# Batch 2 transposed by the DMA crossbar in the start of a fused attention and ReGLU kernel, with a new written order

## The chip, the core and the metric

The kernel runs on one core of a Trainium2 chip. A core has a matrix engine (TensorE, PE in the profile, with its weight loads as PEld), a vector engine (DVE), a scalar engine (ACT), GpSimd (POOL) and SyncE (SP). Each of them takes its instructions in order and waits on semaphores. DMA transfers are issued from SP, ACT and POOL and are carried by 16 DMA engines. Matmuls read SBUF and write PSUM, which has eight banks of 128 x 512 fp32. The metric is the device time of the program in microseconds; lower is better.

## The reference

Two functions are chained. The first is a cross attention between the tokens `x` (8 batches, 8 heads, 512 tokens, 64 features) and a state of 32 rows per head; both directions are computed, and their outputs are concatenated along the rows. The second is a ReGLU feed-forward layer (512 to 1536 to 512).

```python
scores = scale * np.matmul(x, state.transpose(0, 1, 3, 2))     # then softmax over the state rows
xread = np.matmul(a, state)
scores2 = scale * np.matmul(state, x.transpose(0, 1, 3, 2))    # then softmax over the tokens
sread = np.matmul(a2, x)
attn = np.concatenate([xread, sread], axis=2)                  # (B, H, S + Ns, D), to rows of H * D
gate = np.maximum(attn @ w_gate, 0.0)
out = gate * (attn @ w_val) @ w_out
```

Inputs and output are fp32; the kernel computes its matmuls in bf16.

## The kernel before

For a batch `b` the product of the attention with the weights is regrouped: `U[b]` = state times `w_gate` and `w_val` (256 x 1536 each), so that gate and value are `U` times the attention weights. The steps of one batch are these.

- `x` is loaded and brought to bf16 in `xb`. A load by GpSimd can convert on the way (`x_load`, L430, word `dx`); a plain load goes to an fp32 tile `xf` (`x_dma`, L100, word `df`), which an engine then converts (`x_conv`, L144). `x_next` (L438, word `xn`) converts both halves on GpSimd and issues a crossbar transpose from SP into `xT` (`x_trans_dma`, L166).
- `xT` can also come from TensorE: `x_T2` (L188, word `xT2`) makes 16 transposes into PSUM, and `x_out2` (word `xo2`) copies them to SBUF.
- The states come in groups `g` of two batches. `state_conv` (L119, word `stc`) writes them with the unused heads zeroed, in two halves. Then either `state_T` (L127, word `stT`, four transposes on TensorE) and `state_out` (L141, word `sto`) bring them into `stT`, or `state_T_dma` (L133, by the crossbar, from SP) and `state_out_dma` (L137).
- `att_sc` (L201, word `sc`) makes the scores of half the heads, `att_exp` (`ex`) the exponential on ACT, `att_sum` (`nr`) and `att_scale` (`nx`) the softmax on DVE, giving `a_sn`.
- `a_sn` is transposed into `ANS[b]`: by `att_T` (L239, `aT`) and `att_out` (L257, `ao`) through PSUM, or by `att_aT_dma` (L234) from SP.
- `c_unit` and `u_unit` (words `c`, `u`) compute pieces of `U`; `c_out` and `u_out` (`co`, `uo`) copy them out of PSUM.
- `gv` (L331) makes gate and value of one slice of 128 hidden features, four matmuls into two PSUM banks; `relu` on ACT (`re`) and `mult` on DVE (`mu`) give a slice of `hsb`.
- `out_part` (L400, word `o`) is a third of the second layer's matmuls for 128 tokens; `fin_x` (L371, word `of`) copies the sum out and stores it from SP.
- The other direction is `sr_mm` (`sr`), `sr_norm` (`sn`) and a copy of x with a column of ones (`x_pad`, `xp`, on GpSimd); its result is transposed by the crossbar (`sr_T_dma`) and goes through a loop of its own at the end.

The kernel sets its own order. The first 28 slices (all of batches 0 and 1, four of batch 2) follow the string `program` (L456 to L483), a list of words: the name of a step, its arguments, the engine of a copy, and after `@` the PSUM banks. The order of the words is the order in which each engine gets its instructions. `spin` words are matmuls on zeros into a bank of their own, placed in the start. GpSimd's DMA words are, in order: x of batch 1 (the tail of batch 0 stands ahead of the string), fourteen pieces of the two weights (`dw`), x of batch 2, the states (`ds`), the two halves of `w_out` (`do`), and x of batch 3.

From slice 28 on a loop takes over (`first`, L518): one `gv`, `relu`, `mult` and one output part for each slice, and at fixed slices the attention of the next batch, its `U`, the loads and the crossbar transposes. This loop is the same text in both kernels. The output parts lag 18 slices behind.

Buffers that matter here: two of `xf`, four of `xb`, two of `xT`, two of `a_sn`, three of `ANS`, four of the output tile.

Of the kernel before, what the change touches and what calls it, by code (L numbers as in the profile page):

```python
# [16 lines left out]
def kernel(  # L17
# [9 lines left out]
    nc = tc.nc  # L27

    B, H, S, D = x.shape
# [40 lines left out]
    stT = const.tile([128, B, NJ, 64], BF16, name="stT")  # L70
# [6 lines left out]
    xf, xb, xT, e_sn, a_sn, ANS, U, hsb, sr_sb = {}, {}, {}, {}, {}, {}, {}, {}, {}  # L77
    copy = {"act": nc.scalar.copy, "dve": nc.vector.tensor_copy, "pool": nc.gpsimd.tensor_copy}

    given, turn = [], {"r": 0, "o": 1}  # L80

    def bank(name, kind="r"):

# [12 lines left out]
    def state_dma(eng, lo, hi):  # L96
        src = state.rearrange("(g b) h (m i) d -> (b h m) g i d", b=2, i=4)
        eng.dma_start(out=st_f[:, lo // 2:hi // 2], in_=src[:, lo // 2:hi // 2])

    def x_dma(b, engs):  # L100
        xf[b] = xin.tile([128, H, NC, D], FP32, name="xf", tag="xf")
        n = H // len(engs)
        for i, eng in enumerate(engs):
            src = x[b, i * n:(i + 1) * n].rearrange("h (p c) d -> p h c d", c=NC)
            eng.dma_start(out=xf[b][:, i * n:(i + 1) * n], in_=src)
# [262 lines left out]
    def out_rows(b, tsub):  # L368
        return out[b * SP: b * SP + S].rearrange("(p q) m -> q p m", q=NC)[tsub]

    def fin_x(b, tsub, eng="act"):  # L371
        o_sb = opool.tile([128, d_model], FP32, name="o_sb", tag="o_sb")
        copy[eng](out=o_sb, in_=held["o", b, tsub])  # L373
        n = 2 if b == B - 2 and tsub < 2 else 1
        for i in range(n):
            rows = slice(128 // n * i, 128 // n * (i + 1))
            nc.sync.dma_start(out=out_rows(b, tsub)[rows], in_=o_sb[rows])
# [26 lines left out]
    def out_piece(b, i):  # L404
        out_part(b, i)
        if i % 3 == 2:
            fin_x(b, i // 3)
# [37 lines left out]
    def spin(n, cols=512):  # L445
        for i in range(n):
# [2 lines left out]


    steps = {"spin": spin, "stc": state_conv, "stT": state_T, "sto": state_out, "xc": x_conv_pair, "xT": x_T, "xT2": x_T2, "xo2": x_out2, "on": lambda: nc.gpsimd.memset(xa[:, :, :, D:D + 1], 1.0), "dw": w_load, "dx": x_load, "ds": lambda: state_dma(nc.gpsimd, 2, B), "do": wo_dma,
             "df": lambda b: x_dma(b, (nc.gpsimd,)), "xo": x_out,
             "sc": att_sc, "ex": att_exp, "nr": att_sum, "nx": att_scale, "aT2": att_T2, "ao2": att_out2, "aT": att_T, "ao": att_out,
             "c": c_unit, "co": c_out, "u": u_unit, "uo": u_out, "gv": gv, "re": relu, "mu": mult, "o": out_part,
             "of": fin_x, "xn": x_next, "xp": x_pad, "sr": sr_mm, "sn": sr_norm}
    program = """  # L456
    dx.1.0.2 dx.1.1.2 stc.0.0.act stc.0.1.act xc.0.0.dve dw.0.0.128 spin.7 stT.0@4 xc.0.1.act dw.1.0.128 on xT.0.0@2
    sto.0.dve xT.0.1@5 xo.0.0.dve dw.0.128.128 xo.0.1.dve dw.1.128.128 spin.1 sc.0.0@3 dw.0.256.256 ex.0.0 xT.0.2@0
    xT.0.3@1 xo.0.2.dve dw.1.256.256 xo.0.3.act nr.0.0 spin.2 sc.0.1@6 dw.0.512.256 xT2.1.0@4 ex.0.1 nx.0.0
    xo2.1.0.act nr.0.1 dw.1.512.256 spin.2 xT2.1.1@2 xo2.1.1.dve sc.1.0@5 dw.0.768.256 ex.1.0 nx.0.1 dw.1.768.256  # L460
    spin.2 c.0.0.128@30 sc.1.1@1 co.0.0.128.0.act nr.1.0 aT.0.1@6 co.0.0.128.1.act dw.0.1024.256 aT.0.0@4 ex.1.1
    ao.0.0.dve ao.0.1.act dw.1.1024.256 spin.1 c.0.128.128@25 c.1.0.128@30 nr.1.1 co.0.128.128.1.act gv.0.0@14
    co.0.128.128.0.act co.1.0.128.1.act nx.1.0 re.0.0 dw.0.1280.256 c.1.128.128@65 nx.1.1 gv.0.1@20 co.1.0.128.0.act
    co.1.128.128.0.act mu.0.0 co.1.128.128.1.act aT.1.1@7 re.0.1 dw.1.1280.256 aT.1.0@1 ao.1.1.act c.0.256.256@36
    ao.1.0.dve c.1.256.256@54 mu.0.1 co.0.256.256.0.act gv.1.1@21 dx.2.0.1 co.1.256.256.0.act co.0.256.256.1.dve
    re.1.1 gv.1.0@73 co.1.256.256.1.act mu.1.1 ds re.1.0 c.1.512.256@05 c.0.512.256@62 co.1.512.256.1.dve
    co.1.512.256.0.act gv.1.2@41 co.0.512.256.1.act mu.1.0 do.0.6 co.0.512.256.0.act gv.0.3@70 re.1.2 xp.1 gv.1.5@52
    re.0.3 mu.1.2 re.1.5 mu.0.3 gv.0.4@36 mu.1.5 re.0.4 xp.0 c.1.768.256@47 c.0.768.256@15 mu.0.4 co.1.768.256.0.act
    gv.0.2@03 co.0.768.256.0.act co.1.768.256.1.dve re.0.2 gv.0.5@26 do.6.12 co.0.768.256.1.act mu.0.2 gv.1.7@41 df.3
    re.0.5 re.1.7 mu.0.5 gv.0.7@70 mu.1.7 re.0.7 gv.1.3@53 mu.0.7 re.1.3 gv.1.4@24 mu.1.3 re.1.4 gv.1.6@61 mu.1.4  # L470
    re.1.6 c.1.1280.256@70 c.0.1280.256@53 mu.1.6 co.1.1280.256.0.act c.1.1024.256@24 stc.1.0.pool xT2.2.0@6
    co.0.1280.256.0.act co.1.1024.256.0.dve xT2.2.1@1 co.0.1280.256.1.act co.1.1024.256.1.dve stc.1.1.pool
    c.0.1024.256@75 xo2.2.1.act gv.0.10@23 co.1.1280.256.1.dve stc.3.1.pool co.0.1024.256.1.dve re.0.10 gv.1.9@40
    co.0.1024.256.0.act xo2.2.0.dve stc.2.0.pool re.1.9 gv.0.6@12 mu.0.10 stc.3.0.pool re.0.6 mu.1.9 gv.0.11@57 mu.0.6
    stc.2.1.pool re.0.11 gv.0.8@64 mu.0.11 re.0.8 stT.1@3 gv.1.10@10 mu.0.8 sto.1.act re.1.10 sc.2.0@2 o.0.0@7 ex.2.0
    mu.1.10 nr.2.0 sc.2.1@5 gv.0.9@34 ex.2.1 re.0.9 nx.2.0 o.0.1 mu.0.9 gv.1.11@12 nr.2.1 xn.3 re.1.11 o.0.2 mu.1.11
    o.0.3@6 nx.2.1 of.0.0.act u.2.0.1024@05 u.2.1.512@34 uo.2.0.1024.0.dve uo.2.0.1024.1.act sr.0@1 sr.1@2
    uo.2.1.512.1.act sn.0 u.2.0.0@50 sn.1 xp.2 xp.3 o.0.4 uo.2.0.0.0.act uo.2.0.0.1.dve aT.2.1@4 uo.2.1.512.0.dve
    o.0.5 ao.2.1.act o.0.6@7 of.0.1.act u.2.1.0@12 u.2.0.512@50 uo.2.1.0.0.act uo.2.1.0.1.dve u.2.1.1024@34 o.0.7
    uo.2.1.1024.0.act uo.2.1.1024.1.dve uo.2.0.512.0.act gv.1.8@12 uo.2.0.512.1.dve re.1.8 aT.2.0@3 o.0.8 mu.1.8  # L480
    ao.2.0.dve o.0.9@6 of.0.2.act gv.2.0@45 re.2.0 gv.2.2@01 mu.2.0 re.2.2 gv.2.1@23 mu.2.2 re.2.1 gv.2.3@45 mu.2.1
    re.2.3 mu.2.3
    """  # L483
    for word in program.split():
        word, _, banks = word.partition("@")
# [56 lines left out]
    for g in range(first, NF * (B + 1)):  # L542
        b, jf = divmod(g, NF)
# [47 lines left out]
```

The softmax here doesn't subtract the row's maximum and nothing guards it: scores larger than these inputs give would overflow.

## Time and profile before

| | us |
|---|---|
| median of 3 runs | 223.0 (222.78 to 223.1) |
| the profiled execution | 223.1 |
| its span | 221.3 |
| PE busy | 216.4 (98%) |
| DVE busy | 129.9 (59%) |
| ACT busy | 125.1 (57%) |
| POOL busy | 48.6 (22%) |

The span runs from the first to the last instruction of the profiled execution; its own time is 1.8 us longer. The profile's rows have the start, the duration, the engine, the line, the operation, the tiles, how many instructions were merged, and in brackets the idle time before them and what ended it. Ends of matmuls are modelled, so that two groups may overlap; the distance from one start to the next is the time that a group takes. The TensorE clock was granted in full throughout. The page's rows by slices divide the span in 40 parts of 5.5 us.

### The profile page before, as it was taken

The numbers are of one execution on the slowest core, as the hardware profiler recorded it, in microseconds if no ns is written. First come the engines' busy times: TensorE is split into PE (matmuls) and PEld (weight loads), VectorE is DVE, ScalarE is ACT, GpSimd is POOL, SyncE is SP. The second block draws the span as 40 slices with busy tenths as digits, with TensorE's granted clock in tenths as the row PEclk, the third lists the DMA queues.
The fourth block names the chain that finished last, engine by engine and source line by source line (L and its number), as shares of the span: only waits on it lengthen the run. The fifth ranks groups of instructions, "written<-read, shape, count | busy, mean of one in ns | idle before, by whom it ended". The sixth has DMA issues, their size and how long they took to land.

```text
span 221.3 us, 4871 instructions
## 1 busy us (share of the span) xinstructions
PE 216.4 (98%) x1955; PEld 105.9 (48%) x1955; DVE 129.9 (59%) x229; ACT 125.1 (57%) x238; POOL 48.6 (22%) x54
## 2 busy tenths in 40 slices
PE   7899999999999999999999999999999999999994
PEld 3554455444544453444444444445444445666544
DVE  2697898965787558564767378646875333222100
ACT  5599887565667547465565456645654544222222
POOL 8777845460001524006000700000000000000000
PEclk9999999999999999999999999999999999999999
DMA  7999999172058582691169113511311112211132
GB/s 154 174 194 196 199 241 277 49 192 77 16 116 241 110 275 78 141 264 52 49 146 280 58 47 95 110 41 50 96 50 53 49 47 47 52 56 71 66 95 95
DMA packets 40343, 26.01 MB, mean 118 GB/s; under 512 B 21536, under 2 KB 35744, under 8 KB 40320
## 3 DMA queue, kind: packets, MB, share of 16 engines
q1 hardware_dynamic: 27456, 17.47, 28.4%
q0 software_dynamic: 11968, 7.47, 21.9%
q10 hardware_dynamic: 896, 0.75, 1.3%
q8 instruction: 15, 0.25, 0.5%
q14 instruction: 8, 0.07, 0.1%
HBM read 18.35 MB, written 8.91 MB: 123 GB/s over the span
## 4 chain that ended last, share of the span: by engine, by line
PE 88%; DMA 7%; DVE 1%; ACT 1%; POOL 1%; issue 1%; DVEq 0%; POOLq 0%; ACTq 0%
PE o_ps L365 37%; PE gv_ps L328 36%; PE gv_ps L345 5%; PE up L303 4%; DMA xb<-in_x_dram 3%; DMA hs_sb<-sn 3%; PE upc L303 2%; PE sc_ps L209 1%; PE sr_ps L273 1%; DMA out_dram<-o_sb 1%; PE xT_ps L195 1%; PE aT_ps L244 1%; DVE h_sb L356 1%; ACT o_sb L373 1%; POOL xb L427 0%
## 5 line engine op out<-in xcount | busy, mean ns | idle before, releaser
L365 PE MATMUL o_ps<-wo_sb,h_sb 128*128 128x512 bf16 x372 | 94.8, 379 | 0.0
L328 PE MATMUL gv_ps<-ans,U 128*128 128x512 bf16 x384 | 94.0, 379 | 0.0
L356 DVE TENSOR_TENSOR h_sb<-gv_ps,g_sb 128x512 bf16<-128x512 f32 x96 | 65.1, 689 | 44.1 <-ACT g_sb L352 42.2
L352 ACT ACTIVATE g_sb<-gv_ps 128x512 bf16<-128x512 f32 (+1 forms) x108 | 62.5, 581 | 45.2 <-PE gv_ps L328 34.4
L328 PEld LDWEIGHTS <-U 128*128 128x128 bf16 x384 | 36.2, 98 | 42.2 <-issue 0.4
L365 PEld LDWEIGHTS <-h_sb 128*128 128x128 bf16 x372 | 35.2, 98 | 39.7 <-issue 1.6
L373 ACT COPY o_sb<-o_ps 128x512 f32<-128x512 f32 x31 | 18.3, 590 | 17.2 <-PE o_ps L365 17.2
L313 ACT CAST U<-up 128x512 bf16<-128x512 f32 x36 | 19.0, 593 | 11.7 <-PE up L303 11.7
L313 DVE CAST U<-up 128x512 bf16<-128x512 f32 x36 | 22.7, 684 | 4.0 <-PE up L303 3.7
L151 POOL CAST xb<-xf 128x1024 bf16<-128x1024 f32 x10 | 10.1, 1042 | 67.5 <-DMA xf<-in_x_dram 67.5
L265 POOL COPY xa<-xb 128x2048 bf16<-128x2048 bf16 (+1 forms) x9 | 15.2, 1711 | 1.3 <-issue 1.0
L222 DVE TENSOR_REDUCE cs<-e_sn 128x16 f32<-128x512 bf16 x16 | 10.9, 682 | 7.4 <-ACT e_sn L216 7.4
L356 DVE TENSOR_TENSOR hs_sb<-gv_ps,g_sb 128x256 bf16<-128x256 f32 x12 | 5.1, 425 | 15.3 <-PE gv_ps L345 10.1
L216 ACT ACTIVATE e_sn<-sc_ps 128x512 bf16<-128x512 f32 x16 | 9.6, 600 | 7.8 <-PE sc_ps L209 7.7
L228 DVE TENSOR_TENSOR a_sn<-e_sn,rc 128x512 bf16<-128x512 bf16 x16 | 11.7, 736 | 0.4
L303 PEld LDWEIGHTS <-stT 64*32 64x32 bf16 x512 | 6.0, 90 | 10.6 <-issue 9.3
L323 ACT CAST U<-upc 128x512 bf16<-128x512 f32 (+1 forms) x21 | 9.7, 534 | 0.6 <-PE upc L303 0.6
L303 PE MATMUL up<-wg_sb,stT 64*32 64x512 bf16 x144 | 8.0, 382 | 0.2 <-DVE h_sb L356 0.2
L209 PEld LDWEIGHTS <-xT 128*128 128x128 bf16 x128 | 5.9, 99 | 4.1 <-DVE xT L186 0.8
L303 PE MATMUL up<-wv_sb,stT 64*32 64x512 bf16 x144 | 7.6, 380 | 0.0
L345 PE MATMUL gv_ps<-br,wg_sb 128*128 128x256 bf16 x48 | 7.2, 273 | 0.0
L345 PE MATMUL gv_ps<-br,wv_sb 128*128 128x256 bf16 x48 | 7.2, 273 | 0.0
(62 smaller groups left out, 119.4 us busy)
## 6 DMA issues: line engine op xcount, KB each, us to landing
out_dram<-o_sb SPq DMA_DIRECT2D x29, 256.0 KB, 2.3
xf<-in_x_dram SPq DMA_DIRECT2D x4, 1024.0 KB, 6.4
wo_sb<-in_moe_w_out_dram POOLq DMA_DIRECT2D x2, 768.0 KB, 13.4
wg_sb<-in_moe_w_gate_dram POOLq DMA_DIRECT2D x5, 256.0 KB, 8.9
wv_sb<-in_moe_w_val_dram POOLq DMA_DIRECT2D x5, 256.0 KB, 9.5
xf<-in_x_dram POOLq DMA_DIRECT2D x1, 1024.0 KB, 15.0
xb<-in_x_dram POOLq DMA_DIRECT2D x3, 256.0 KB, 6.5
out_dram<-o_sb SPq DMA_DIRECT2D x5, 128.0 KB, 2.3
```

Source lines behind the costliest of these rows:

```text
L151: copy[eng](out=xb[b][:, :, hs].rearrange("p c h d -> p h c d"), in_=xf[b][:, hs])
L222: nc.vector.reduce_sum(out=cs, in_=e_v, axis=AX.X)
L228: {"dve": nc.vector, "pool": nc.gpsimd}[eng].tensor_tensor(out=by_pair(a_sn[b], jp).rearrange("p r (j n) -> p r j n", n=Ns), in0=e_v, in1= ...
L265: nc.gpsimd.tensor_copy(out=v[:, hs:hs + src.shape[1]], in_=src)
L303: nc.tensor.matmul(dst[parity][32 * j:32 * j + 32], stT[r:r + 64, b, j, 32 * parity:32 * parity + 32], wsb[r:r + 64, j, lo:lo + n], start= ...
L313: copy[eng](out=U[b][:, w, kc, lo:lo + 512], in_=held["u", b, w, lo][kc])
L328: nc.tensor.matmul(ps[w], U[b][:, w, kc, f0:f0 + 128], ANS[b][:, kc].rearrange("p c t -> p (c t)"), start=(kc == 0), stop=(kc == NK - 1))
L345: nc.tensor.matmul(ps[w][:, 0:nt], wsb[:, j, f0:f0 + 128], br[:, j].rearrange("p b n -> p (b n)"), start=(j == 0), stop=(j == NJ - 1))
L352: nc.scalar.activation(out=g_sb[:, 0:n], in_=ps[0][:, 0:n], func=AF.Relu)
L356: nc.vector.tensor_tensor(out=dst, in0=ps[1][:, 0:n], in1=held["g", b, jf][:, 0:n], op=ALU.mult)
L365: nc.tensor.matmul(held["o", b, tsub], src[:, jf, tsub * 128:(tsub + 1) * 128], wo_sb[:, jf], start=(jf == 0), stop=(jf == NF - 1))
L373: copy[eng](out=o_sb, in_=held["o", b, tsub])
```

## The change

Four things differ.

1. x of batch 2 is loaded in fp32 (`df.2` instead of `dx.2.0.1`), converted by GpSimd and transposed by the crossbar (`xn.2` instead of `xT2.2.0`, `xT2.2.1` and two `xo2`).
2. The states of batches 2 and 3 (group 1) are transposed by the crossbar: `sd.1` and `sdo.1.dve` instead of `stT.1@3` and `sto.1.act`.
3. `a_sn` of batch 2 is transposed by the crossbar: `ad.2` instead of `aT.2.0`, `aT.2.1` and two `ao`.
4. The string has a new order of all its words, with other engines for some copies and other banks. The loop is the same; `fin_x` stores seven row blocks in halves (the four of batch 6, three of batch 5) instead of two.

The functions behind the new words stood in the kernel already:

```python
def x_next(b):
    x_conv(b, 0, "pool")
    x_conv(b, 1, "pool")
    x_trans_dma(b)

def state_T_dma(g):
    t = held["st", g] = spare[:, 512 * g:512 * g + 512].rearrange("p (i t) -> p i t", i=4)
    nc.sync.dma_start_transpose(out=t, in_=st_b[:, g % 3].rearrange("p i h d -> p (i h d)"))
```

The diff, with the string cut to its first lines and to the stretches with the words named above:

```diff
-    given, turn = [], {"r": 0, "o": 1}
+    given, turn = [], {"r": 0, "o": 0}
...
-        n = 2 if b == B - 2 and tsub < 2 else 1
+        n = 2 if b == B - 2 or (b == B - 3 and tsub < 3) else 1
...
-             "df": lambda b: x_dma(b, (nc.gpsimd,)), "xo": x_out,
+             "df": lambda b: x_dma(b, (nc.gpsimd,)), "srt": sr_T_dma, "xo": x_out,
...
-             "of": fin_x, "xn": x_next, "xp": x_pad, "sr": sr_mm, "sn": sr_norm}
+             "of": fin_x, "xn": x_next, "ad": att_aT_dma, "sd": state_T_dma, "sdo": state_out_dma, "xp": x_pad, "sr": sr_mm, "sn": sr_norm}
...
-    dx.1.0.2 dx.1.1.2 stc.0.0.act stc.0.1.act xc.0.0.dve dw.0.0.128 spin.7 stT.0@4 xc.0.1.act dw.1.0.128 on xT.0.0@2
-    sto.0.dve xT.0.1@5 xo.0.0.dve dw.0.128.128 xo.0.1.dve dw.1.128.128 spin.1 sc.0.0@3 dw.0.256.256 ex.0.0 xT.0.2@0
...
-    re.1.6 c.1.1280.256@70 c.0.1280.256@53 mu.1.6 co.1.1280.256.0.act c.1.1024.256@24 stc.1.0.pool xT2.2.0@6
-    co.0.1280.256.0.act co.1.1024.256.0.dve xT2.2.1@1 co.0.1280.256.1.act co.1.1024.256.1.dve stc.1.1.pool
...
-    stc.2.1.pool re.0.11 gv.0.8@64 mu.0.11 re.0.8 stT.1@3 gv.1.10@10 mu.0.8 sto.1.act re.1.10 sc.2.0@2 o.0.0@7 ex.2.0
-    mu.1.10 nr.2.0 sc.2.1@5 gv.0.9@34 ex.2.1 re.0.9 nx.2.0 o.0.1 mu.0.9 gv.1.11@12 nr.2.1 xn.3 re.1.11 o.0.2 mu.1.11
...
-    uo.2.1.1024.0.act uo.2.1.1024.1.dve uo.2.0.512.0.act gv.1.8@12 uo.2.0.512.1.dve re.1.8 aT.2.0@3 o.0.8 mu.1.8
-    ao.2.0.dve o.0.9@6 of.0.2.act gv.2.0@45 re.2.0 gv.2.2@01 mu.2.0 re.2.2 gv.2.1@23 mu.2.2 re.2.1 gv.2.3@45 mu.2.1
-    re.2.3 mu.2.3
+    dx.1.0.2 dx.1.1.2 stc.0.0.act stc.0.1.dve dw.0.0.128 xc.0.0.dve spin.7 stT.0@2 xT.0.0@3 xc.0.1.dve dw.1.0.128 on
+    sto.0.act xT.0.1@0 xo.0.0.act dw.0.128.128 xo.0.1.act dw.1.128.128 spin.1 sc.0.0@4 dw.0.256.256 ex.0.0 xT.0.2@1
...
+    co.0.256.256.0.dve aT.1.1@5 aT.1.0@0 co.1.256.256.0.act mu.0.1 gv.0.3@31 df.2 co.1.256.256.1.act ao.1.0.dve
+    ao.1.1.act mu.0.0 gv.0.2@74 re.0.3 ds re.0.2 mu.0.3 c.1.512.256@20 c.0.512.256@56 co.1.512.256.0.act gv.1.0@37
...
+    co.1.1280.256.1.act co.0.1280.256.1.dve re.0.9 gv.1.2@23 co.1.1280.256.0.dve re.1.2 gv.1.9@64 mu.0.9 xn.2 re.1.9
+    mu.1.2 gv.1.8@75 mu.1.9 re.1.8 gv.1.5@12 mu.1.8 stc.1.1.pool re.1.5 gv.1.10@06 mu.1.5 stc.1.0.pool re.1.10
+    gv.0.10@34 mu.1.10 re.0.10 stc.3.1.pool gv.0.8@75 mu.0.10 re.0.8 stc.3.0.pool gv.1.1@12 mu.0.8 sd.1 re.1.1
+    stc.2.1.pool gv.1.11@06 mu.1.1 re.1.11 stc.2.0.pool gv.1.7@34 mu.1.11 re.1.7 gv.1.6@75 mu.1.7 re.1.6 gv.0.11@12
+    sdo.1.dve mu.1.6 re.0.11 sc.2.1@0 o.0.0@6 mu.0.11 ex.2.1 nr.2.1 u.2.0.1024@34 u.2.0.512@51 uo.2.0.1024.0.act
+    u.2.0.0@02 o.0.1 uo.2.0.512.1.dve uo.2.0.0.0.act uo.2.0.1024.1.dve o.0.2 uo.2.0.512.0.dve sc.2.0@3 nx.2.1
+    of.0.0.act sr.1@1 sr.0@0 xn.3 ex.2.0 uo.2.0.0.1.dve o.0.3@7 sn.1 nr.2.0 o.0.4 sn.0 xp.2 xp.3 o.0.5 nx.2.0 o.0.6@6
+    ad.2 of.0.1.dve o.0.7 u.2.1.512@45 u.2.1.0@32 uo.2.1.512.0.act uo.2.1.512.1.dve u.2.1.1024@10 o.0.8
+    uo.2.1.1024.1.act uo.2.1.1024.0.dve uo.2.1.0.1.act o.0.9@7 uo.2.1.0.0.dve of.0.2.act gv.2.3@45 re.2.3 gv.2.1@01
+    mu.2.3 re.2.1 gv.2.2@23 mu.2.1 re.2.2 gv.2.0@45 mu.2.2 re.2.0 mu.2.0
```

## The prediction

> **What bounds the kernel now.** I read the busy rows first, then TensorE's instructions in order of time, then the chain of waits, then the queues of GpSimd and SyncE and the DMA traffic between 28 and 41 us. The rows that carry the argument, from the page's slices and from the order of time on PE:
>
> ```profile
> PE   7899999999999999999999999999999999999994
> DMA  7999999172058582691169113511311112211132
> ...
> 30.29 1.08 PE L195 MATMUL xT_ps<-id,xb 128*64 128x128 bf16 x32
> 35.97 0.39 PE L130 MATMUL stT_ps<-id,st_b 128*128 128x128 bf16 x4
> 45.33 0.39 PE L244 MATMUL aT_ps<-id,a_sn 128*128 128x128 bf16 x4
> 49.89 0.39 PE L244 MATMUL aT_ps<-id,a_sn 128*128 128x128 bf16 x4
> 51.84 4.48 PE L328 MATMUL gv_ps<-ans,U 128*128 128x512 bf16 x20
> ```
>
> TensorE is the bound: from about 11 us on one group starts as the last one stops issuing, and the chain of waits is 88% PE. So a change pays only by taking PE work away, and costs only where PE is made to wait. At 51.84 the last four gv units of the written order begin, with everything else of it done; behind them both kernels run the same loop. I therefore compare one instant: when those four can begin.
>
> The second view, queues and traffic, shows what new waits would meet:
>
> ```profile
> 17.68 0.89 POOL L435 DMA_DIRECT2D xb<-in_x_dram  x1 [0.37 <-DMA wg_sb<-in_moe_w_gate_dram]
> 30.54 5.44 POOL L125 TENSOR_SCALAR st_b<-st_f,odd 128x256 bf16<-128x256 f32 x6 [3.77 <-DMA st_f<-in_state_dram]
> 40.90 2.02 POOL L151 CAST xb<-xf 128x1024 bf16<-128x1024 f32 x2 [4.92 <-DMA xf<-in_x_dram]
> 42.95 2.11 SPq L168 DMA_TRANSPOSE xT<-xb  x1
> ...
> q0 software_dynamic: 2027, 2.98, 103.2%
> ```
>
> The last row is the DMA queues' view of 28 to 41 us: GpSimd's queue alone fills all 16 engines there. It carries, in order, batch 2, the states, W_out in two halves and batch 3. The issues asked one by one land at 29.5 (17.68 + 11.8), 30.4, 34.2, 38.0 and 40.9. The crossbar has not been used yet: its first transpose is issued at 42.95, when that traffic is over.
>
> **What the Trainium skill says.** "DMA: Bandwidth & Descriptors", section "Issuing engines are not separate DMA queues": queues of all engines run on the same 16 DMA engines and interleave. Same page, "Queues, rings and completion order": each engine goes round robin between the queues that have work, a packet at a time. This trace shows one full queue at a time, never a transpose beside GpSimd's loads, so neither is tested here; both decide the case. "Advanced Engine Details and Errata", "X-Bar Transpose (TRN2)", expects 350 to 400 GB/s of a transpose. The trace disagrees: the fastest xT (512 KB) lands 4.4 us after issue, the fastest ans (256 KB) 3.0 to 3.1, so 256 KB cost 1.3 us, about 200 GB/s. I split by that: xT 2.6 us of data, ans 1.3, a state group (128 KB) 0.65, each after a fixed 1.75.
>
> **The change, part by part.**
>
> *PE work removed.* From start to the next start: the 32 transposes of x take 1.01 us (30.29 to 31.30), the four of the states 0.23, the two groups of a_sn 0.23 and 0.22. Sum 1.69.
>
> *The first 19 us.* The states' second half goes to DVE, the copies of stT and of the first two xT from DVE (0.43 each) to ACT (0.59), the first spins grow from 15 to 16 matmuls, and the transposes of a_sn of batch 0 come before the first U units. I followed the three engine queues by their durations. The ACT copies are about 0.4 late for the first scores, but x's tail (DMA, 7.36) gates all again. At 11.5 aT.0 is 0.7 earlier. Then ACT has the copies of xT, exp, ans and four U tiles in a row, so the first gv starts near 13.95 instead of 13.45, with one U unit already ahead of it. The weights of columns 512 to 767 land at about 19.0 in both. I take 0.25 us lost at that point; bounds: nothing, and 0.5. The extra spin lies in this stretch, while PE waits for weights and casts; uncovered it costs 0.2.
>
> *When PE reaches the scores of batch 2.* At 42.80 the old order has done all U units, 23 gv, 4 output parts, and the transposes and scores of batch 2. The new one needs 24 gv and nothing else of these before sc.2.1: 42.80 + 0.87 - 4 x 0.865 - 1.01 - 0.23 - 0.47 = 38.5, with the start 38.75. From there to the last four gv: ten output parts 8.65, two scores 0.47, sr 0.64, six U units 1.79: 11.55, so 50.3 unhindered. That is 1.5 us before 51.84, the whole possible gain.
>
> *Batch 2 in fp32.* The load reads the same 1 MB, writes 1 MB instead of 0.5. Batch 3, loaded so, takes 40.9 - 38.0 = 2.9 us; the cast load took 2.7 (from the last W_val landing at 26.8). I take the same 29.5; at most 0.3 more. Two casts on GpSimd at 1.04 end at 31.6. GpSimd's later queue (states 5.44 us, then the casts of batch 3 at about 41) is free to absorb 2.1 us, since the states of groups 2 and 3 are needed only in the loop. Moving xp.0 behind the second W_out half (1.9 us earlier to issue) changes nothing: that queue is full anyway.
>
> *Crossbar transpose of batch 2 (on SP).* Issued at 31.6; SP is empty before. Alone it lands 4.4 later, 36.0. The state group: two stc at 0.92 end at 33.4, SP is still issuing until 33.7; it follows in the ring, data at the earliest to 36.7, and its copy, now on DVE in front of two mults, takes 0.6 at most (ACT's row for it), 37.3. That would be 1.4 us ahead of 38.75. But GpSimd's queue fills the engines until 39.6. Shared half and half, x takes 5.2 of data and lands at 38.6, the states 1.3 more, 39.9, copied at 40.5: sc.2.1 waits 1.75. PE is in order, so all behind it waits: 52.05.
>
> *What this pushes.* If the transposes' 2.6 + 0.65 us come out of the same engines, the second half of W_out lands near 41.2 (needed at 41 or later: 0.2 at most) and batch 3 near 44.1. Its casts, 2.05, end at 46.15; only then does SP issue xT of batch 3 (2.1 us on SP), and **ad.2 stands behind it in SP's queue**, whatever the state of a_sn (ready near 46). Landing of ad.2: 46.15 + 1.75 + 2.6 + 1.3 = 51.8 at the transpose's best. At this very place the trace before has 6.2 instead of 4.4 for xT, beside output stores: 53.6. Middle 52.7. gv.2.3, the first of the last four, needs it. The removed 0.45 us of PE transposes had no such queue.
>
> *Outputs split.* Seven row blocks of batches 5 and 6 are stored in halves instead of two: five more SP issues at 0.34. They fall after 170 us, where SP has ten issues in 36.7 us. Nothing; uncovered 1.7.
>
> **Likeliest: shared engines.** The four gv begin at the later of 52.05 and 52.7: 0.86 later than 51.84. Against its own execution: 223.1 (span 221.3 and 1.8 around it) + 0.86 = 224.0; that execution lies 0.1 over the median 223.0, so 223.9. Its own range: 51.8 to 54 gives 223.0 to 225.1.
>
> **Rivals.**
> *Hidden (faster).* Transposes slip into idle slots of the engines, because the loads wait on HBM and a transpose stays inside SBUF. For it: in the W_out stretch 206 GB/s are written, under the 389 that batch 3 reaches; the alone-landing leaves 1.4 us. Against: the DMA row is at nine tenths or more there, and batch 3 only has to slip by 2 us for ad.2 to come after 50.3. Price: the start at 50.3, -1.5: 221.5. It decides if batch 3 lands by about 42.6 (42.6 + 2.05 + 5.65 = 50.3). This is the case on the other side.
>
> *Starved (much slower).* Turns go by small pieces, and a transpose's rows are shorter than a load's, so x crawls until GpSimd's queue drains at about 40.9. At a fifth of the rate it has 1.6 of 2.6 us by then; it lands near 42, the states 43, copied 43.6: PE waits 4.85, +3.3. With no progress until then, +5.0. Middle +4.2: 227.2. For it: the full queue; against: nothing in the trace shows row sizes per turn.
>
> *No change.* ad.2 lands at 51.8, its best: the gain of 1.5 is eaten exactly. This is the lower end of the likeliest.
>
> **Chances.** Shared 0.50 (0.14 of it within 0.2%), hidden 0.28 (0.02 of it within), starved 0.22. A measurement of this kernel tells about 0.2% (0.45 us) from none. So faster 0.26, within 0.16, slower 0.58. The range leaves out the most hidden and the most starved ends: 221.5 to 228.0.
>
> **What will show it.** The removed PE groups at L195 (32 of 64), L130 and L244 gone. PE idle or weight loads waiting in front of sc.2.1 near 39 us for xT or the state copy on DVE: none (hidden), about 2 us (shared), over 4 (starved). The landing of batch 3: 41, 44. ad.2's issue right behind the second xT transpose and a wait of gv.2.3 on ans. I am wrong if PE also waits elsewhere between 19 and 38 us: DVE has there about 17 us of work for 19 us, and 1 us of slack at the banks I followed.

## The result, and the profile after

| | before | after |
|---|---|---|
| median | 223.05 us (222.78 to 223.1) | 235.61 us (234.7 to 446.44) |
| ratio, 95% interval | | 1.0552 [1.0519, 1.0585] |
| profiled execution, its span | 223.1, 221.3 | 235.75, 234.0 |

The change makes the kernel 5.5% slower; 223.9 was predicted and 228.0 was the upper end. In one execution of the changed kernel, the one of 446.44 us, TensorE ran at less than half its rate from beginning to end (0.47 us from one 512-column matmul to the next instead of 0.22), so the profile shown here as "after" is that of another execution of the same code, of 235.75 us, from the session of the experiments below (medians there: 235.03 us, and 224.37 before).

The rows by slices of after, to be held against the two shown of before:

```profile
PE   7789998079999999689999999999999999999995
PEclk9999999659999999999999999999999999999999
DMA  7999999905705759159116911541141212121133
```

One slice of PE is nearly empty (the eighth, 41 to 47 us), and TensorE's clock is down there and in the next. Before, PE had nine tenths from the third slice to the last but one.

The order of time on PE, DVE, SP and GpSimd around that hole, after (start, duration, engine, line, operation, tiles, count, and in brackets the idle time before it and what ended it):

```profile
28.50 11.40 PE L328 MATMUL gv_ps<-ans,U 128*128 128x512 bf16 x51
48.33 0.59 PE L209 MATMUL sc_ps<-stT,xT 128*128 128x64 bf16 x8 [8.43 <-DVE stT L138]
61.82 2.54 PE L328 MATMUL gv_ps<-ans,U 128*128 128x512 bf16 x11
...
47.57 0.61 DVE L138 COPY stT<-hs_sb 128x512 bf16<-128x512 bf16 x1 [8.47 <-DMA hs_sb<-st_b]
...
32.69 9.07 SPq L168 DMA_TRANSPOSE xT<-xb  x1
41.81 2.52 SPq L135 DMA_TRANSPOSE hs_sb<-st_b  x1
...
46.02 2.02 POOL L151 CAST xb<-xf 128x1024 bf16<-128x1024 f32 x2 [7.95 <-DMA xf<-in_x_dram]
```

PE has done its 24 `gv` units at 39.90 and stands until 48.33 for `sc.2.1`. It waits for the copy of the states on DVE, and that waits for the states' transpose. SP needed 9.07 us to issue the transpose of x (2.11 before, for batch 3), so the states' transpose began only at 41.81. By the queue's view x landed 14.4 us after its issue, at 47.1, and the states 5.7 after theirs, at 47.5. The last row is batch 3's load: 46.02, where before has 40.90.

The granted clock by stages, after and before (columns: stretch, its length, then busy time and instructions of PE, PEld, DVE, ACT, POOL, then clock, DMA share, GB/s):

```profile
38.50:42.20 3.70, 1.40 (x7) 0.43 (x5) 0.59 (x1) 1.19 (x2) 0.00 (x0) 1.00 1.27 196
42.20:52.50 10.30, 3.95 (x37) 1.45 (x39) 3.57 (x7) 1.59 (x3) 2.02 (x2) 0.50 0.58 54
52.50:62.00 9.50, 9.29 (x131) 4.48 (x132) 7.56 (x15) 3.32 (x7) 4.20 (x2) 1.00 0.62 138
```

```profile
42.20:52.50 10.30, 10.30 (x156) 4.68 (x154) 6.71 (x13) 6.04 (x12) 4.46 (x3) 1.00 0.42 103
```

The clock fell to half while PE stood and stayed there until 52.46, four microseconds into its work.

The spans differ by 12.7 us; the medians of that session differ by 10.7, so about 2 us lie with these two executions. The 12.7 goes in this way, from the rows above, the two spans and the prediction's sums (38.5 and 11.55):

| | us |
|---|---|
| PE reaches `sc.2.1` at 39.90 instead of the 38.5 of the sum (the weights of columns 256 to 511 landed later in this execution: PE waited for them at 16.27 and 16.95) | +1.40 |
| PE work removed and reordered: 51.84 less the 50.05 that 38.5 and 11.55 give | -1.79 |
| wait for the states and x at `sc.2.1` | +8.43 |
| from `sc.2.1` to the last four `gv`: 61.82 - 48.33 = 13.49 instead of 11.55, at half clock in part | +1.94 |
| the loop behind them: 172.2 instead of 169.5, PE waits between 94 and 101 us | +2.72 |
| sum | 12.70 |

The experiments ask why both transposes took so long, whether one of them would have done so alone, and what the wait costs beside its own length. "Before" in each is the kernel before, timed on the same chip in the same session.

### The profile page after: what moved, and what is told of

Same layout as the page of the kernel before. It is cut to its first block, busy times and chain, and to the rows that moved or that the text cites. A ratio compares the mean times of both kernels' runs of the same rounds, so it can differ in the third digit from the quotient of the medians.

```text
span 444.7 us, 4794 instructions
## 1 busy us (share of the span) xinstructions
PE 440.4 (99%) x1912; PEld 156.5 (35%) x1912; DVE 133.9 (30%) x232; ACT 127.6 (29%) x231; POOL 51.1 (11%) x56
## 3 DMA queue, kind: packets, MB, share of 16 engines
q0 software_dynamic: 11200, 8.00, 10.7%
## 4 chain that ended last, share of the span: by engine, by line
PE 98%; DMA 1%; POOL 0%; issue 0%; DVE 0%; POOLq 0%; DVEq 0%
PE o_ps L365 42%; PE gv_ps L328 40%; PE gv_ps L345 5%; PE up L303 4%; PE sc_ps L209 2%; DMA xb<-in_x_dram 1%; PE o_ps L394 1%; PE upc L303 1%; PE warm_ps L447 1%; PE sr_ps L273 1%; PE xT_ps L195 0%; PE aT_ps L244 0%; PE xT_ps L182 0%; POOL id masks.py:199 0%; DVE o_sb L397 0%
## 5 line engine op out<-in xcount | busy, mean ns | idle before, releaser
L328 PE MATMUL gv_ps<-ans,U 128*128 128x512 bf16 x384 | 192.2, 680 | 0.0
L365 PE MATMUL o_ps<-wo_sb,h_sb 128*128 128x512 bf16 x372 | 190.6, 678 | 0.0
L328 PEld LDWEIGHTS <-U 128*128 128x128 bf16 x384 | 54.6, 145 | 112.9 <-issue 111.8
L365 PEld LDWEIGHTS <-h_sb 128*128 128x128 bf16 x372 | 54.4, 149 | 108.0 <-issue 103.5
L265 POOL COPY xa<-xb 128x2048 bf16<-128x2048 bf16 (+1 forms) x9 | 15.7, 1765 | 32.2 <-PE sr_ps L273 31.9
L222 DVE TENSOR_REDUCE cs<-e_sn 128x16 f32<-128x512 bf16 x16 | 10.9, 684 | 22.7 <-ACT e_sn L216 22.7
L345 PE MATMUL gv_ps<-br,wg_sb 128*128 128x256 bf16 x48 | 14.0, 450 | 0.0
L345 PE MATMUL gv_ps<-br,wv_sb 128*128 128x256 bf16 x48 | 13.7, 449 | 0.0
L209 PEld LDWEIGHTS <-xT 128*128 128x128 bf16 x128 | 9.4, 126 | 9.5 <-issue 7.9
L303 PE MATMUL up<-wv_sb,stT 64*32 64x512 bf16 x144 | 12.0, 654 | 0.0
L365 PE MATMUL o_ps<-wo_sb,hs_sb 128*128 128x512 bf16 x24 | 11.5, 684 | 0.0
L303 PE MATMUL up<-wg_sb,stT 64*32 64x512 bf16 x144 | 11.5, 619 | 0.0
## 6 DMA issues: line engine op xcount, KB each, us to landing
wo_sb<-in_moe_w_out_dram POOLq DMA_DIRECT2D x2, 768.0 KB, 15.5
```

Source lines behind the costliest of these rows:

```text
L209: nc.tensor.matmul(ps[:, :, c, jj], xT[b][:, c, 2 * jp + jj], stT[:, b, 2 * jp + jj], start=True, stop=True)
L265: nc.gpsimd.tensor_copy(out=v[:, hs:hs + src.shape[1]], in_=src)
L303: nc.tensor.matmul(dst[parity][32 * j:32 * j + 32], stT[r:r + 64, b, j, 32 * parity:32 * parity + 32], wsb[r:r + 64, j, lo:lo + n], start= ...
L328: nc.tensor.matmul(ps[w], U[b][:, w, kc, f0:f0 + 128], ANS[b][:, kc].rearrange("p c t -> p (c t)"), start=(kc == 0), stop=(kc == NK - 1))
L345: nc.tensor.matmul(ps[w][:, 0:nt], wsb[:, j, f0:f0 + 128], br[:, j].rearrange("p b n -> p (b n)"), start=(j == 0), stop=(j == NJ - 1))
L365: nc.tensor.matmul(held["o", b, tsub], src[:, jf, tsub * 128:(tsub + 1) * 128], wo_sb[:, jf], start=(jf == 0), stop=(jf == NF - 1))
```

## The experiments

### The change again, and the wait filled

*a0_same* is the changed kernel itself.

> The changed kernel itself once more, for its profile. Theory S (starved crossbar): the transpose of x of batch 2 lands 13 to 14 us after its issue, PE stands still for about 7 us in front of sc.2.1, and its clock falls to half and stays there for some us of work after it; in all 235 to 236 us. Theory O (the new order): PE loses its 12 us in many small waits between 15 and 55 us, no single one over 3 us.

Measured: 235.03 us, ratio 1.0468 [1.0417, 1.0519]. Its profile is the one shown above.

*a1_busy* keeps the change and gives PE 34 matmuls on zeros ahead of `sc.2.1`.

```diff
+    def keep_busy(n):
+        ps = bank("keep_ps")
+        for i in range(n):
+            nc.tensor.matmul(ps, warm[:, 0:128], warm, start=True, stop=True)
...
-    sdo.1.dve mu.1.6 re.0.11 sc.2.1@0 o.0.0@6
+    sdo.1.dve mu.1.6 re.0.11 kb.34@0 sc.2.1@0 o.0.0@6
```

> 34 matmuls on zeros (7.3 us at full clock) are put in front of sc.2.1, so that PE works while it waits. Theory S with a clock part: the wait stays, the half clock behind it goes, 229 to 232 us. S without a clock part: 235 to 236 us, as the changed kernel. Theory O: about 7 us more, 242 us.

Measured: 230.51 us, ratio 1.0282 [1.0249, 1.0315]. The order of time on PE, and the stages, of a1_busy:

```profile
46.85 0.39 PE L209 MATMUL sc_ps<-stT,xT 128*128 128x64 bf16 x8 [0.18 <-DVE stT L138]
58.45 4.48 PE L328 MATMUL gv_ps<-ans,U 128*128 128x512 bf16 x20
```

```profile
42.20:52.50 10.30, 9.80 (x140) 4.81 (x141) 6.29 (x13) 2.75 (x5) 2.75 (x3) 1.00 0.43 62
```

The clock stays at 1.00, and from `sc.2.1` to the four `gv` it takes 11.60 us, which is the 11.55 of the prediction. So half clock costs the change 1.9 us in this stretch. `sc.2.1` still starts at 46.85: the transposes are as late with PE busy as with PE idle. The spans differ by 5.6 us (the medians by 4.5): 1.9 is the clock, 1.5 that the transposes landed earlier in this execution, 2.2 the loop, which has one wait of 0.54 us here instead of two of 1.3.

### One transpose at a time, in the order of before

*b2_sd* is the kernel before with nothing but the states of batches 2 and 3 (128 KB) by the crossbar.

```diff
-    stc.1.1.pool
+    stc.1.1.pool sd.1
...
-    re.0.8 stT.1@3 gv.1.10@10 mu.0.8 sto.1.act
+    re.0.8 gv.1.10@10 mu.0.8 sdo.1.act
```

> The kernel before with one part of the change alone: the states of group 1 by the crossbar (128 KB, issued near 32.4 us). Theory S, as the changed kernel without the transpose of x showed (8.7 us to landing): it lands near 41, sc.2.0 is reached near 37 and waits 4 to 5 us, plus the clock: 1.015 to 1.03. If so small a transpose slips through once it stands alone in the old order: 0.998 to 1.002.

*b3_x* is the kernel before with nothing but batch 2 loaded in fp32, converted and transposed as in the change.

```diff
-    gv.1.1@21 dx.2.0.1
+    gv.1.1@21 df.2
...
-    stc.1.0.pool xT2.2.0@6
+    xn.2 stc.1.0.pool
...
-    xT2.2.1@1
-    xo2.2.1.act
-    xo2.2.0.dve
```

> The kernel before with one part alone: batch 2 in fp32, converted by GpSimd and transposed by the crossbar (issued near 31.7 us). Theory S: lands after 13 to 14 us, near 45; sc.2.0 reached near 36 waits 8 to 9 us, plus the clock: 1.04 to 1.055, about the whole of the change. If the states' transpose and the new order carry much of the loss: 1.01 to 1.025.

Measured: b2_sd 234.2 us, ratio 1.0429 [1.0395, 1.0463], above the 1.03 that was expected at most; b3_x 235.94 us, ratio 1.0538 [1.0472, 1.0603]. Order of time of b2_sd on PE, SP and GpSimd:

```profile
45.01 0.58 PE L209 MATMUL sc_ps<-stT,xT 128*128 128x64 bf16 x8 [6.97 <-ACT stT L138]
...
33.45 1.30 SPq L135 DMA_TRANSPOSE hs_sb<-st_b  x1
...
44.21 2.02 POOL L151 CAST xb<-xf 128x1024 bf16<-128x1024 f32 x2 [7.19 <-DMA xf<-in_x_dram]
```

The same of b3_x:

```profile
46.18 0.61 PE L209 MATMUL sc_ps<-stT,xT 128*128 128x64 bf16 x8 [7.55 <-DMA xT<-xb]
...
32.54 8.43 SPq L168 DMA_TRANSPOSE xT<-xb  x1
...
44.99 2.02 POOL L151 CAST xb<-xf 128x1024 bf16<-128x1024 f32 x2 [7.07 <-DMA xf<-in_x_dram]
```

Either transpose alone costs about what the whole change costs; the two losses don't add, since both waits end together. About 1 us of each loss lies ahead of the wait: in these executions PE came to it at 38.04 and 38.63, where before begins its scores at 37.06 (b3_x had a wait of 1.27 us for the last rows of batch 0 and half clock from 8.5 to 11.9 us). And size hardly matters: 128 KB landed 10.9 us after issue (44.35), 512 KB 13.6 (46.14). What the two have in common is the last row of each: the transpose lands when batch 3's load lands, within 0.2 us for the states and 1.2 us after it for x. That is when GpSimd's queue has run dry.

### The same transposes with nobody waiting

To part the transfer from the wait, *b5_dummy_st* issues the states' transpose in the kernel before, into a scratch region that nothing reads, and leaves TensorE's transposes as they were. *b4_dummy_x* does so with three quarters of batch 2 (384 KB).

```diff
-    stc.1.1.pool
+    stc.1.1.pool sd.1
```

```diff
+    def extra():
+        nc.sync.dma_start_transpose(out=spare[:, 512:2048].rearrange("p (i t) -> p i t", t=128),
+                                    in_=xb[2].rearrange("p c h d -> p (h c d)")[:, 0:1536])
...
-    stc.1.0.pool xT2.2.0@6
+    stc.1.0.pool xt xT2.2.0@6
```

> The kernel before with one more crossbar transpose: the states of batches 2 and 3 (128 KB), issued where the change issues it, into a scratch region that nothing reads; the PE transposes of before stay. Theory (wait): it lands 8 to 11 us after its issue as it did when sc.2.0 waited for it, batch 3's load lands 2 to 3 us later than before, and the kernel takes 223.2 to 225 us (ratio 0.999 to 1.005). Rival A (traffic): ratio at or above 1.02. Rival B: it lands within 5 us.

> The kernel before with one more crossbar transpose: three quarters of batch 2's x (384 KB), issued where the change issues its own, into a scratch region that nothing reads; the PE transposes of before stay. Theory (the transpose starves beside GpSimd's loads, and the kernel's loss is the wait for it): it lands 9 to 14 us after its issue, its data late, batch 3's load lands some 3 us later than the 40.9 of before, and since no engine waits for it the kernel takes 223.5 to 225.5 us (ratio 1.000 to 1.006), TensorE at full clock between 36 and 52 us. Rival A (the transposes' traffic itself, not the wait, costs the time: it slows other engines' accesses to SBUF or delays the loads of later batches): ratio at or above 1.02. Rival B (a transpose is only slow because of the changed load of batch 2): it lands within 6 us.

Measured: b5_dummy_st 225.43 us, ratio 1.0063 [1.0043, 1.0083]; b4_dummy_x 228.26 us, ratio 1.0151 [1.0092, 1.0211].

The queue's view of b5_dummy_st, from the issue at 32.5 in stretches of 2 to 2.5 us (32.5 to 35, 35 to 37, 37 to 39, 39 to 41, 41 to 43; packets, MB, time as a share of the 16 engines). q0 is GpSimd's queue, q1 here the transpose alone, in rows of 256 bytes:

```profile
q0 software_dynamic: 515, 0.52, 125.3%
...
q0 software_dynamic: 342, 0.52, 114.0%
q1 hardware_dynamic: 56, 0.01, 4.2%
...
q0 software_dynamic: 151, 0.45, 93.9%
q1 hardware_dynamic: 193, 0.05, 20.5%
...
q0 software_dynamic: 66, 0.24, 39.8%
q1 hardware_dynamic: 223, 0.05, 13.0%
...
q0 software_dynamic: 44, 0.16, 22.1%
q1 hardware_dynamic: 71, 0.02, 4.0%
```

And the issue of that stretch, with the time to landing:

```profile
hs_sb<-st_b SPq DMA_TRANSPOSE x1, 11.1
```

With nobody waiting it is as slow as in b2_sd, 11.1 us. In the first 2.5 us not one of its 512 rows moves (before's first xT, issued at 42.95 with the queue empty, has none until 43.9 and 108 by 44.4). Later both queues crawl together: from 39 to 41 us 0.24 and 0.05 MB in 2 us, and the engines are not even full, 39.8 and 13.0%. Before moved 352 to 389 GB/s from 37 to 39 us, in the tail of that load. So a transfer that alone takes 0.65 us of data holds up GpSimd's loads too. The issues of batch 3 and of the second half of W_out with their times to landing, b5_dummy_st and then before:

```profile
xf<-in_x_dram POOLq DMA_DIRECT2D x1, 1024.0 KB, 17.8
wo_sb<-in_moe_w_out_dram POOLq DMA_DIRECT2D x1, 768.0 KB, 15.3
```

```profile
xf<-in_x_dram POOLq DMA_DIRECT2D x1, 1024.0 KB, 15.0
wo_sb<-in_moe_w_out_dram POOLq DMA_DIRECT2D x1, 768.0 KB, 12.9
```

Two other kernels with no transpose in this place, b1_ad and b6_ad_split below, have 15.6 and 15.5 for batch 3 and 13.5 for W_out. For b4_dummy_x the two are 20.0 and 17.4. Even b5_dummy_st, at 1.0063 a little above the 1.005 that was expected, has a wait for W_out on PE:

```profile
40.52 0.59 PE L365 MATMUL o_ps<-wo_sb,h_sb 128*128 128x512 bf16 x2 [0.49 <-DMA wo_sb<-in_moe_w_out_dram]
```

This is where the expectation of b4_dummy_x fell short: it was to take 225.5 at most, and its ratio lies between that and the 1.02 of the rival in which the traffic itself costs the time. Its order of time on PE, from the longest of its four executions (231.36 us; the others took 225.59 to 228.36), so that the sizes are this execution's:

```profile
42.75 0.59 PE L365 MATMUL o_ps<-wo_sb,h_sb 128*128 128x512 bf16 x2 [2.65 <-DMA wo_sb<-in_moe_w_out_dram]
56.48 4.48 PE L328 MATMUL gv_ps<-ans,U 128*128 128x512 bf16 x20
```

The delayed W_out becomes a wait of its own, and the clock falls to 0.56 after it (stretch 43 to 46 us): the four `gv` come at 56.48 instead of 51.84. So the transfer has two prices. The engine that needs the transposed data waits for it (1.043 for the states when waited for, 1.006 when not), and whoever needs the loads beside it waits for these. In the change the second is hidden behind the first: W_out's second half landed at 42.8, before `sc.2.1` was released.

### The loads moved away, and the transposes taken out

*a3_hold_ad* is the change with the second half of W_out and batch 3 issued only behind the states' transpose; `ad.2` goes ahead of batch 3's casts, which then come later.

```diff
-    co.0.768.256.1.act do.6.12 gv.0.5@70
+    co.0.768.256.1.act gv.0.5@70
...
-    gv.0.6@42 df.3 co.1.1024.256.1.act
+    gv.0.6@42 co.1.1024.256.1.act
...
-    mu.0.8 sd.1 re.1.1
+    mu.0.8 sd.1 re.1.1 do.6.12 df.3
...
-    sr.0@0 xn.3 ex.2.0
+    sr.0@0 ex.2.0
...
-    xp.2 xp.3 o.0.5
+    xp.2 o.0.5
...
-    ad.2 of.0.1.dve
+    ad.2 xn.3 xp.3 of.0.1.dve
```

> The changed kernel with the second half of W_out and batch 3 issued by GpSimd only after the transposes of batch 2 and of the states are issued, and with ad.2 ahead of batch 3's transpose on SP. Theory S: with the first W_out half done at about 34 us, the transpose lands 5 to 8 us after issue instead of 13 to 14, sc.2.1 waits 1 us or less, W_out's second half lands at 42 to 43 and costs 1 to 2 us at the second output part: 1.000 to 1.012 of the kernel before. If the transpose is slow by itself (SP, the crossbar), it still takes 13 us: 1.04 or more.

Measured: 228.25 us, ratio 1.0166 [1.0131, 1.0201], where at most 1.012 was expected. Order of time of a3_hold_ad on PE, SP and GpSimd, and the landing of the held loads:

```profile
41.43 0.39 PE L209 MATMUL sc_ps<-stT,xT 128*128 128x64 bf16 x8 [2.16 <-DVE stT L138]
54.61 4.48 PE L328 MATMUL gv_ps<-ans,U 128*128 128x512 bf16 x20
...
32.05 3.03 SPq L168 DMA_TRANSPOSE xT<-xb  x1
35.12 1.27 SPq L135 DMA_TRANSPOSE hs_sb<-st_b  x1
...
35.59 0.89 POOL L115 DMA_DIRECT2D wo_sb<-in_moe_w_out_dram  x1
36.48 0.90 POOL L105 DMA_DIRECT2D xf<-in_x_dram  x1
...
xf<-in_x_dram POOLq DMA_DIRECT2D x1, 1024.0 KB, 10.4
wo_sb<-in_moe_w_out_dram POOLq DMA_DIRECT2D x1, 768.0 KB, 8.4
```

With only the first half of W_out beside it, x lands 5.8 us after issue instead of 14.4, and SP issues it in 3.03 us instead of 9.07. The states also take 5.8: the held loads begin while they are under way, and `sc.2.1` still waits 2.16 us. The clock falls for 3.4 us. But neither transpose waits for the held loads to end: x lands at 37.9 and the states at 40.9, the loads at 44.0 and 46.9. So in these runs a transpose is held until the loads issued before it have landed (here the first half of W_out, at 35.1); loads issued after it slow it, but it lands ahead of them.

*a4_peT* gives x of batch 2 back to TensorE, right ahead of `sc.2.1`, and keeps the states' and a_sn's transposes on the crossbar. *a5_order* gives the states back as well: what is left of the change is its order, the fp32 load and the transpose of a_sn.

```diff
-    gv.1.9@64 mu.0.9 xn.2
+    gv.1.9@64 mu.0.9 xh.2
...
-    re.0.11 sc.2.1@0
+    re.0.11 xT2.2.0@3 xo2.2.0.act xT2.2.1@4 xo2.2.1.dve sc.2.1@0
```

```diff
-    mu.0.8 sd.1 re.1.1
+    mu.0.8 re.1.1
...
-    re.1.7 gv.1.6@75
+    re.1.7 stT.1@0 sto.1.dve gv.1.6@75
...
-    sdo.1.dve mu.1.6
+    mu.1.6
```

(`xh` is `x_next` without the transpose; the second diff is against a4_peT.)

> The changed kernel with x of batch 2 transposed by TensorE after its cast (32 transposes and two copies in front of sc.2.1); states and a_sn of batch 2 still by the crossbar. Theory S: the long wait is gone, what is left is the state group's own landing, 5 us or less after its issue at 34 us: 223 to 225 us. Theory O: stays above 230 us.

> The new order alone as far as it goes: x and the states of batch 2 transposed by TensorE at the places of the new order, x still loaded in fp32 and converted by GpSimd, a_sn of batch 2 still by the crossbar. Theory S: nothing waits for a crossbar transpose beside loads any more: 0.997 to 1.006 of the kernel before. Theory O: 1.015 or more.

Measured: a4_peT 231.43 us, ratio 1.0316 [1.0279, 1.0352]; a5_order 224.89 us, ratio 1.0048 [1.0027, 1.0069]. Order of time of a4_peT on PE and GpSimd, then of a5_order on PE:

```profile
44.76 0.61 PE L209 MATMUL sc_ps<-stT,xT 128*128 128x64 bf16 x8 [4.29 <-DVE xT L198]
...
42.32 2.08 POOL L151 CAST xb<-xf 128x1024 bf16<-128x1024 f32 x2 [4.88 <-DMA xf<-in_x_dram]
```

```profile
41.74 0.41 PE L209 MATMUL sc_ps<-stT,xT 128*128 128x64 bf16 x8 [0.79 <-DVE xT L198]
53.34 4.48 PE L328 MATMUL gv_ps<-ans,U 128*128 128x512 bf16 x20
```

In a4_peT the states' transpose was issued at 33.87 and landed at 42.57, again as batch 3's load ended, and not the 5 us or less after issue that was expected. So a4_peT missed its 223 to 225 us and came out where the order of the words would have been to blame (above 230); a5_order tells the two apart. The releaser named is DVE's copy of xT; it stood behind the copy of the states in DVE's queue, so the states are still what is waited for. Without any crossbar beside the loads (a5_order) 2.7% more is gone (1.0316 to 1.0048), and of the change's loss 0.5% is left: a wait of 0.79 for the copies of xT and 11.60 us behind it. So the two transposes are nine tenths of the loss: 4.7% become 0.5%.

### The part of the change that pays

*b1_ad* is the kernel before with a_sn of batch 2 by the crossbar (`ad.2` behind `nx.2.1`, `aT.2` and `ao.2` gone). *b6_ad_split* adds halved stores in all of batches 5 and 6 and in one block of batch 4: nine row blocks, where the change has seven and before two.

```diff
-    nx.2.1 of.0.0.act
+    nx.2.1 ad.2 of.0.0.act
...
-    aT.2.1@4
-    ao.2.1.act
-    aT.2.0@3
-    ao.2.0.dve
```

```diff
-        n = 2 if b == B - 2 and tsub < 2 else 1
+        n = 2 if b in (B - 2, B - 3) or (b == B - 4 and tsub < 1) else 1
```

> The kernel before with one part of the change alone: a_sn of batch 2 by the crossbar, 0.45 us of PE transposes removed. Issued near 45 us, after GpSimd's loads are done. Theory S: it lands in 4 to 6 us, before 51.4, so -0.4 us: 222.6. If crossbar transposes cost PE waits wherever they stand, 223.5 to 226.

> The kernel before with a_sn of batch 2 transposed by the crossbar after the loads have ended (as in b1_ad), and the outputs of batch 5 and the first of batch 4 written in two halves as in the change. b1_ad alone gave 0.9986. Expected 0.996 to 1.000: the split outputs cost nothing, and at most the mean wait for an output buffer changes. Rival: the split itself costs, 1.002 or more, and is then a part of the loss that a5_order still has.

Measured: b1_ad 223.92 us, ratio 0.9986 [0.9972, 0.9999]; b6_ad_split 223.36 us, ratio 0.9972 [0.9949, 0.9995]. This transpose is issued after the loads have ended and is not waited for. b6_ad_split is 0.3% faster than before; whether the halved stores add to b1_ad's gain can't be told, since the intervals overlap, but nothing shows that they cost.

## Why the prediction was wrong

The step that failed is "Shared half and half, x takes 5.2 of data and lands at 38.6". It lands at 47.1 in after, at 46.1 as the only transpose in b3_x. Two things in it were wrong. The crossbar gets no half share: none of its rows move in the first 2.5 us (b5_dummy_st), and the transpose is complete only about when the loads issued before it have landed, 1.1 us after batch 3 for x in after. And the share was taken from a fixed sum of traffic, where in the traces the sum shrinks: the loads end at 42 to 46 us instead of 40.9. So the wait of 1.75 became 8.43. The rival "starved" had the right kind ("With no progress until then"), but it took 40.9 for the end of the queue and priced no clock, and so had the four `gv` 3.3 to 5.0 us later, where they came 9.98 later (61.82 instead of 51.84).

"Queues, rings and completion order" in the Trainium skill's "DMA: Bandwidth & Descriptors", which stood behind the half share, has each engine go round robin between its queues, a packet at a time. The runs don't show such turns, as the profile counts packets: b5_dummy_st moved 515 of the loads and none of the transpose in its first stretch, 66 and 223 from 39 to 41 us. The same section says that a semaphore's increment waits for every earlier write of its DMA engine, across queues. That fits the 128 KB landing together with batch 3 in three kernels (within 0.3 us in b2_sd, a4_peT and b5_dummy_st), and a3_hold_ad's states taking 5.8 us once new loads had begun, but no run here tested it alone. What in the DMA engines slows both queues stays open. No run issued a plain transfer from SP in this place, so it is not shown either that it takes a transpose to be held up so.

The other steps, one by one:

- *PE work removed, 1.69, and 11.55 from `sc.2.1` to the four `gv`*: the 11.55 is right: 11.60 in a1_busy and in a5_order, at full clock. Of the 1.69 only the 0.45 of a_sn was tried alone, and b1_ad's 0.14% is 0.3 us.
- *The wait at its own length only*: wrong. The clock after a wait was not priced; a1_busy shows 1.9 us of it. "TensorE: Matmul & The Clock Gate" in the Trainium skill, "Part 1: The HAM clock gate", has the clock at half after an idle window of about 3.4 us. The traces agree on the length of a window: the falls lasted 10.24 us in after (42.22 to 52.46), 6.83 in b2_sd (43.43 to 50.26) and 3.41 in a3_hold_ad (41.86 to 45.27), three, two and one times 3.41. They differ on how long PE must stand: waits of 2.16 us (a3_hold_ad) and 2.65 (b4_dummy_x), shorter than a window, were followed by a fall too, and one of 0.79 (a5_order) was not.
- *The states follow x in the ring*: right, and SP's own issue of x, 9.07 us, came on top. But without x the states still landed at 44.35 (b2_sd), where the prediction has 39.9 with x ahead of them; this was not foreseen.
- *The first 19 us, 0.25 lost*: not shown. PE reached `sc.2.1` 1.15 us later than the sum's 38.75 in after, but only 0.42 later in a1_busy (39.17), so most of it belongs to the execution; before, too, took 224.37 in that session and 223.05 in the first.
- *Batch 2 in fp32 costs at most 0.3*: right. Its casts begin at 30.64, 12.1 us after the issue at 18.51, where the converting load took 11.8.
- *W_out near 41.2, batch 3 near 44.1*: too early. 42.8 and 46.0.
- *`ad.2` gates the four `gv`*: not seen. It was issued at 57.61, and the `gv` at 61.82 show no wait; PE was later than it.
- *Outputs split: nothing*: nothing is seen against it (b6_ad_split, with nine blocks halved).
- *The loop behind is the same*: not quite. It has 2.7 us more in after, from waits at 94 to 101 us, which the other kernels with late loads show in part (0.54 in a1_busy, 1.36 in b4_dummy_x). Why they grow was not tried.

## What to carry to other kernels

In these kernels a crossbar transpose that was issued behind loads in GpSimd's queue landed about when those loads had landed, whether it had 128 or 512 KB, and the loads came later too; expect this, and place the transpose where the queue is empty or ahead of the loads (a3_hold_ad), or leave the work on TensorE. Ask of each new wait of PE not only how long it is, but whether it is long enough to bring the clock down (2.16 us was, 0.79 was not), and price the work behind it at half rate. A transpose that nobody waits for is the way to tell the price of a transfer from the price of a wait.

## What the runs showed of the hardware that was not expected

- A transpose of 128 KB took 8.7 to 11.1 us from issue to landing behind GpSimd's loads (a4_peT, b2_sd, b5_dummy_st), and 2.4 at its best alone (a state group in before). One of 512 KB took 13.3 to 14.4 (a1_busy, b3_x, after), and 4.4 alone. With most of the loads held back both took 5.8 (a3_hold_ad).
- SP is itself held while it issues: 9.07 us for x in after, 8.43 in b3_x, 3.03 in a3_hold_ad, 2.11 at the end of the loads in before. Whatever is behind it in SP's queue waits as long.
- 128 KB of transposed rows delayed the load of batch 3 beside them: it landed 17.2 and 17.8 us after issue (b2_sd, b5_dummy_st), where before, b1_ad and b6_ad_split have 15.0 to 15.6. In a4_peT it is less, 16.3 against 15.7 in a5_order. Meanwhile the two queues kept the DMA engines busy for only 53% of 39 to 41 us (b5_dummy_st).
- A wait of PE of 2.16 us was followed by 3.41 us of half clock (a3_hold_ad), and 34 matmuls on zeros in a wait of about 7.5 us kept the clock at 1.00 (a1_busy).
